# Two experts held to 192 rows, their second tile multiplied with high and low halves side by side

## The chip, the core and the metric

The program runs on one core of one Trainium2 chip. The metric is the device time of one execution in microseconds (us). Engines: PE is TensorE's matmul side and PEld its weight load, DVE is VectorE, ACT is ScalarE, POOL is GpSimd, SP only issues transfers. SBUF is the core's working memory; PSUM is the memory that matmuls write, used here in banks of 128 partitions x 512 floats.

## What is computed

Three stages on 2 x 768 tokens: banded attention, a mixture of eight experts (one expert for each token, with a sticky choice), and a gated feed-forward layer. The middle one is what the change touches:

```python
def _moe_ref(x, w_gate, w_local, w1, w2):          # x 2 x 768 x 512, 8 experts, w1 512 x 1024, w2 1024 x 512
    ...
            fresh_e = int(np.argmax(logits[b, s]))
            if s == 0 or local_gate[b, s] < 0.5:
                e = fresh_e
            else:
                e = prev_e if prev_e >= 0 else fresh_e
            prev_e = e
            ...
            h = np.maximum(x[b, s] @ w1[e], 0.0)
            out[b, s] = p[e] * (h @ w2[e])
```

Then `k = relu(xk @ w_k)`, `v = k*k @ w_v`, `out = sigmoid(xr @ w_r) * v` for all tokens.

## The kernel before, in words

**Precision.** Each operand of a large matmul is kept as two numbers, a high part (rounded for the one-pass mode F32R) and the rest, the low part; a product is three matmuls: high x high, high x low, low x high (`mm3`, lines 633 to 635). Weights arrive from DRAM in chunks of 128 x 1024 floats (512 KB, `wraw`); ACT writes the high part (`w_hi1`, line 617, two halves) and DVE the low part (`w_lo_all`, line 626, `wlo`). An expert has eight chunks: 0 to 3 for its first layer, 4 to 7 for its second.

**Places.** Routing counts the tokens of each expert and ranks them. Place `p` of the order of work (r = 0 to 7 in the code) takes the expert with rank `PLACES[p]`. Each place has a fixed number of rows, `CAPS`: the first 384, the third 320, the others 256. If an expert has more tokens than its place holds, a flag is set and the whole result is computed again by a slow general program at the end. Places 3 and 5 (`SHORT`) take the two smallest experts: 128 rows always, and 128 more behind a branch.

**One ordinary expert (r = 1, 2, 4, 6).** First layer, `l1m(r, f)` for f = 0 to 7: weights stand still, the rows of x move through (N = 256 columns, 320 at place 2), 12 matmuls for each f. ACT and DVE take relu of it and split it into high (`hh`) and low (`hl`). Second layer: for each tile of 128 rows, `l2_mm`, 24 matmuls with h standing still and 512 columns of w2 moving; then `y_out` (ACT copies the bank, ACT's queue writes it to `ys`). The third tile of place 2 has 64 rows only; for it `h3` holds high and low part next to each other as one 128-column operand, `l2_both` multiplies it by w2 high and w2 low, 16 matmuls, and `y_both` adds the two halves of the bank (ACT copies one, DVE adds, POOL's queue writes).

**What sets the order.** All is written out by hand; each engine runs its instructions in that order. Between the matmuls of an expert three kinds of small work are dealt out: `W_` issues the next split of weights of a later expert (and, through `pump`, the next loads on SP's queue); `B_` does one step of decoding the last layer's float64 weights ("words"): three DVE instructions for each piece (lines 486, 488, 490), a piece's load being asked for on POOL's queue when the piece two before it is done (`dec_load`, tiles `dwt`, two of them); and `next(late)` does one step of late routing, which turns counts into the row that each token's result has in `ys`. Tables fix how many: `BL[r]` gives `B_` for each f of the first layer and, in the second, one step at every f with `f % BL[r][1] == BL[r][1] // 2` in the first two tiles. Place 4 (`LATE`) runs late routing in place of words, and a matmul of it (line 415, operand `dj`) on PE.

The functions that the change touches:

## Time and profile before

| | us |
|---|---|
| median of three runs | 489.56 (489.03 to 489.94) |
| the profiled execution, whole | 487.52 |
| its span in the trace | 486.0 |
| PE busy in it | 468.6 (96%) |
| DVE busy | 343.7 (71%) |
| ACT busy | 264.9 (55%) |
| experts r = 1 to 7 | 154.94 to 308.05 us of the span |
| last layer | 308.05 to the end |

A matmul's row gives a start and a duration. Since matmuls are pipelined, durations overlap; what a matmul costs in a stream is the distance from its start to the next start, called its pace below. Rows of a timeline are sorted by start. The rows of the section after next are taken from several views of this one execution.

### The profile page before, as it was taken

What the parts mean: (1) busy time and instruction counts of PE and PEld (TensorE: products, weight loads), DVE (VectorE), ACT (ScalarE), POOL (GpSimd) and SP (SyncE); (2) the same over time, 40 slices, a digit from 0 to 9 for tenths busy, and PEclk for the clock granted to TensorE, in tenths of its full rate; (3) what the DMA queues carried; (4) which work ended last, traced back from release to release, by engine and by line L of the source; (5) the groups of instructions that cost most, each with busy time, mean ns of one, the idle gap of its engine ahead of it and who ended that gap; (6) DMA issues with size and microseconds to landing.
All of it is one profiled execution on the core that took longest, in us unless ns stands there. A gap on an engine that the chain in (4) does not pass through costs nothing. (4 is left out here: it accounts for less than half of the span.)

```text
span 486.0 us, 9271 instructions
## 1 busy us (share of the span) xinstructions
PE 468.6 (96%) x3227; PEld 407.2 (84%) x3227; DVE 343.7 (71%) x891; ACT 264.9 (55%) x644; POOL 112.8 (23%) x198
## 2 busy tenths in 40 slices
PE   7999999799999999999999999999999999999994
PEld 5789888678788989879879888797989899898984
DVE  7777796796957866968878968797866768263301
ACT  5877876883526745576666766862433414142320
POOL 4201212112110000000000003052663918162220
PEclk9999999999999999999999999999999999999998
DMA  8996575973685887699699842102836442200001
GB/s 185 284 223 156 146 173 169 277 230 99 252 301 185 315 260 271 196 363 329 220 332 341 273 166 77 54 2 66 325 109 233 154 160 81 72 15 23 22 3 49
DMA packets 76812, 87.42 MB, mean 180 GB/s; under 512 B 50677, under 2 KB 50933, under 8 KB 76757
## 3 DMA queue, kind: packets, MB, share of 16 engines
q1 hardware_dynamic: 68304, 63.28, 41.8%
q0 software_dynamic: 4848, 16.91, 11.0%
q10 hardware_dynamic: 3604, 6.56, 3.6%
q8 instruction: 28, 0.46, 0.4%
q14 instruction: 28, 0.22, 0.1%
HBM read 73.75 MB, written 12.98 MB: 178 GB/s over the span
## 5 line engine op out<-in xcount | busy, mean ns | idle before, releaser
L617 ACT ACTIVATE whi<-wraw 128x512 fp32r<-128x512 f32 x128 | 72.5, 623 | 7.1 <-ACTq L709 2.3
L626 DVE TENSOR_TENSOR wlo<-wraw,whi 128x1024 fp32r<-128x1024 f32 x55 | 66.1, 1218 | 4.3 <-ACT whi L617 3.8
L1456 ACT ACTIVATE sq<-S 128x256 f32<-128x256 f32 x48 | 18.5, 385 | 73.1 <-PE S L635 73.1
L633 PE MATMUL S<-xkh,whi 128*128 128x256 f32 x192 | 54.3, 283 | 0.2 <-ACT whi L617 0.2
L635 PE MATMUL S<-xkh,wlo 128*128 128x256 f32 x192 | 53.3, 278 | 0.2 <-DVE wlo L622 0.2
L634 PE MATMUL S<-xkl,whi 128*128 128x256 f32 x192 | 53.2, 277 | 0.0
L1466 POOL TENSOR_TENSOR kl<-sq,kh 128x256 fp32r<-128x256 f32 x40 | 36.0, 910 | 70.0 <-issue 36.7
L1496 DVE TENSOR_TENSOR o<-O,sig 128x512 f32<-128x512 f32 (+1 forms) x13 | 8.5, 650 | 51.0 <-PE O L635 31.8
L634 PE MATMUL O<-wlo,kh 128*128 128x512 f32 (+1 forms) x104 | 39.2, 377 | 0.3 <-DVE wlo L622 0.3
L635 PE MATMUL O<-whi,kl 128*128 128x512 f32 (+1 forms) x104 | 39.2, 377 | 0.0
L633 PE MATMUL O<-whi,kh 128*128 128x512 f32 (+1 forms) x104 | 38.9, 374 | 0.0
L633 PEld LDWEIGHTS S<-xkh,whi 128*128 128x128 f32 x192 | 36.1, 188 | 0.7 <-ACT whi L617 0.4
L635 PEld LDWEIGHTS S<-xkh,wlo 128*128 128x128 f32 x192 | 36.1, 188 | 0.4 <-DVE wlo L622 0.4
L634 PEld LDWEIGHTS S<-xkl,whi 128*128 128x128 f32 x192 | 36.2, 188 | 0.3
L1457 DVE SCALAR_TENSOR_TENSOR sq<-S,sq 128x256 f32<-128x256 f32 x48 | 20.1, 420 | 15.0 <-ACT sq L1456 14.7
L1465 ACT ACTIVATE kh<-sq 128x256 fp32r<-128x256 f32 x48 | 19.7, 412 | 12.7 <-DVE sq L1457 12.7
L635 PE MATMUL O<-whi,hl 128*128 128x512 f32 x64 | 25.1, 393 | 0.0
L634 PE MATMUL O<-wlo,hh 128*128 128x512 f32 x64 | 25.1, 392 | 0.0
L633 PE MATMUL O<-whi,hh 128*128 128x512 f32 x64 | 25.0, 391 | 0.0
L278 POOL DMA_INDIRECT xs<-X,posi x12 | 12.6, 1053 | 52.8 <-DVE acc L296 20.1
L884 ACT ACTIVATE zbig<-zbig,nm 128x232 f32<-128x232 f32 (+1 forms) x48 | 22.4, 466 | 3.7 <-DVE nm L872 3.7
L634 PEld LDWEIGHTS O<-wlo,kh 128*128 128x128 f32 x104 | 19.6, 188 | 4.6 <-DVE wlo L622 0.8
(446 smaller groups left out, 1409.1 us busy)
## 6 DMA issues: line engine op xcount, KB each, us to landing
wraw<-in_moe_w_dram SPq DMA_DIRECT2D x64, 512.0 KB, 5.2
dwt<-in_moe_w_v_dram POOLq DMA_DIRECT2D x8, 512.0 KB, 4.7
z<-in_moe_w_k_dram SPq DMA_DIRECT2D x8, 512.0 KB
z<-in_moe_w_v_dram SPq DMA_DIRECT2D x8, 512.0 KB, 5.4
ys<-yo ACTq DMA_DIRECT2D x15, 256.0 KB, 6.3
xn<-xs SPq DMA_DIRECT2D x14, 256.0 KB
vn<-in_v_dram SPq DMA_DIRECT2D x12, 256.0 KB, 3.7
dwt<-in_moe_w_k_dram POOLq DMA_DIRECT2D x6, 512.0 KB, 7.6
```

Source lines behind the costliest of these rows:

```text
L278: self.nc.gpsimd.indirect_dma_start(self.xs, bass.IndirectOffsetOnAxis(ap=self.posi[:, t:t + 1], axis=0), X[t], None)
L617: nc.scalar.activation(out=whl[r, c][0][:, sl], in_=raws[r, c][:, sl], func=ACTF.Copy)
L626: nc.vector.tensor_tensor(lo, raws.pop((r, c)), hi.bitcast(F32), op=ALU.subtract)
L633: nc.tensor.matmul(out_, lhsT=ah, rhs=bh, start=first, stop=False)
L634: nc.tensor.matmul(out_, lhsT=ah, rhs=bl, start=False, stop=False)
L635: nc.tensor.matmul(out_, lhsT=al, rhs=bh, start=False, stop=last)
L884: nc.scalar.activation(out=pe, in_=pe, func=ACTF.Exp, scale=-1.0, bias=nm[:, h:h + 1], accum_out=sm[:, h:h + 1])
L1456: nc.scalar.activation(out=sq_, in_=ps[:, 0:TB], func=ACTF.Relu)
L1457: nc.vector.scalar_tensor_tensor(sq_, ps[:, 0:TB], 0.0, sq_, op0=ALU.max, op1=ALU.mult)
L1465: nc.scalar.activation(out=hh, in_=sq_, func=ACTF.Copy)
L1466: (nc.gpsimd if b else nc.vector).tensor_tensor(hl, sq_, hh.bitcast(F32), op=ALU.subtract)
L1496: nc.vector.tensor_tensor(o[:, a:z], ps[:, 0:z - a], sig[b, i][:, a:z], op=ALU.mult)
```

## The change

Places 4 and 6 (the fifth and the seventh expert, `HALF`) hold 128 + 64 rows rather than 256. `PLACES` gives them the ranks 5 and 4 (rather than 3 and 4), and place 7, which keeps 256 rows, rank 3 (rather than 5). Their first layer has 192 moving columns; their second tile is stored as [high | low], is multiplied by `l2_both` and written by `y_both`. The relu and split of a pair of f is done in two calls (128 rows, then 64 rows). Routing gets a further small table, `second` (128 or 64), in place of the constant 128. Words: place 2 takes 8 + 8 steps rather than 6 + 6, place 6 takes 2 + 8 rather than 6 + 8. Late routing starts in the third tile of place 2 (8 steps) rather than in place 4.

```diff
-PLACES = (0, 1, 2, 7, 3, 6, 4, 5)
+PLACES = (0, 1, 2, 7, 5, 6, 4, 3)
+HALF = (4, 6)
-CAPS = [384, 256, 256 + LAST] + [256] * 5
+CAPS = [384, 256, 256 + LAST, 256, P + LAST, 256, P + LAST, 256]
...
-        nc.vector.memset(self.caps[:, 0:1], float(CAPS[0]))
-        nc.vector.memset(self.caps[:, THIRD:THIRD + 1], float(CAPS[THIRD]))
+        for r in (0, THIRD) + HALF:
+            nc.vector.memset(self.caps[:, r:r + 1], float(CAPS[r]))
...
-        for r in (1, 2):
+        for r in (1, 2) + tuple(range(HALF[0] + 1, E)):
             nc.vector.memset(self.bases[:, r:r + 1], float(BASES[r]))
...
+        self.second = c.tile([8, E], F32, name="second")
+        nc.vector.memset(self.second, float(P))
+        for r in HALF:
+            nc.vector.memset(self.second[:, r:r + 1], float(LAST))
...
-        nc.vector.tensor_scalar(nm[:, 0:1], nm[:, 0:1], -float(P), 0.0, op0=ALU.add, op1=ALU.max)
-        yield
+        yield
+        nc.vector.tensor_tensor(b8, self.R, self.second, op=ALU.mult)
+        nc.vector.tensor_reduce(nm[:, 1:2], b8, axis=AX.X, op=ALU.add)
+        yield
+        nc.vector.tensor_scalar(nm[:, 0:1], nm[:, 0:1], nm[:, 1:2], 0.0, op0=ALU.subtract, op1=ALU.max)
...
-                nc.tensor.matmul(ps, lhsT=ts_[f // 4][:, f % 4].rearrange("p s c -> p (s c)"), rhs=w[:, ds_],
+                nc.tensor.matmul(ps, lhsT=ts_[f], rhs=w[:, ds_],
...
-        return LAST if i == 2 else P
+        return LAST if i == 2 or i == 1 and r in HALF else P
...
+        if r in HALF:
+            full = pair["h"][0].rearrange("p (f s c) -> p f s c", f=2, s=2)
+            hs[r, f] = tuple(full[:, odd, j, :] for j in range(2))
+            h3[r, f] = pair["h"][1][:, odd * 2 * LAST:(odd + 1) * 2 * LAST]
+            last = pair["h"][1][:, 0:4 * LAST].rearrange("p (f s c) -> p f s c", f=2, s=2)
+            if odd:
+                both_ps = pair["ps"].rearrange("p (f c) -> p f c", f=2)
+                for t_, a, z in ((full, 0, P), (last, P, N)):
+                    relu_split(t_[:, :, 0, :], t_[:, :, 1, :], both_ps[:, :, a:z])
+            return
...
-    BL = {1: ((0, 0, 0, 0, 1, 0, 1, 0), 4), 2: ((1, 1, 1, 0, 1, 1, 1, 0), 3), 6: ((1, 1, 1, 0, 1, 1, 1, 0), 2)}
+    BL = {1: ((0, 0, 0, 0, 1, 0, 1, 0), 4), 2: ((1,) * 8, 2), 6: ((1, 0, 1, 0, 0, 0, 0, 0), 2)}
...
+                elif m == LAST:
+                    steps = l2_both(r, ps, [h3[r, f] for f in range(KF)])
...
                     if r == LATE:
                         next(late, None)
-                    elif i < 2 and f % BL[r][1] == BL[r][1] // 2:
+                    elif i == 2:
+                        next(late, None)
+                    elif f % BL[r][1] == BL[r][1] // 2:
                         B_(1)
-                if i == 2:
+                if m == LAST:
                     y_both(rp, ps, BASES[r] + TILES[r][i] * P, m)
```

Line numbers of the changed kernel are 7 or 8 higher at the places quoted below (634 for 626, 641 to 643 for 633 to 635, 681 for 673, 750 for 742, 494 to 498 for 486 to 490).

PE, place 4, the start of the second tile's second layer, before (`hh` and `hl` are high and low of h, `O` the bank):

```order
L633 MATMUL O_3663<-whi_4_3343,hh_0_3389 128x512
L634 MATMUL O_3663<-wlo_4_3344,hh_0_3389 128x512
L635 MATMUL O_3663<-whi_4_3343,hl_0_3390 128x512
L633 MATMUL O_3663<-whi_4_3343,hh_0_3389 128x512
L634 MATMUL O_3663<-wlo_4_3344,hh_0_3389 128x512
L635 MATMUL O_3663<-whi_4_3343,hl_0_3390 128x512
```

The end of the first tile and the start of the second, after; here `hh` holds both parts of the first tile and `hl` both parts of the second:

```order
L643 MATMUL O_3618<-whi_7_3541,hh_6_3576 128x512
L681 MATMUL O_3707<-whi_4_3384,hl_0_3431 128x512
L681 MATMUL O_3707<-wlo_4_3385,hl_0_3431 128x512
L681 MATMUL O_3707<-whi_4_3384,hl_0_3431 128x512
L681 MATMUL O_3707<-wlo_4_3385,hl_0_3431 128x512
```

Two matmuls stand for each f where three stood: 16 for the tile rather than 24. In the first layer the count stays, and the size changes from 128x256 to 128x192.

DVE, place 2, from the second tile's second layer to place 3's first h, before (`wlo_3` to `wlo_6` are weights of place 3; 486, 488, 490 are the three steps of a piece of words; `yo` is the third tile's result; `ehl` is the low part of place 3's h):

```order
L626 TENSOR_TENSOR wlo_3_3045<-wraw_3_2831,whi_3_3044 128x1024
L486 TENSOR_SCALAR z_2254<-dwt_3021 128x512
L626 TENSOR_TENSOR wlo_4_3077<-wraw_4_2876,whi_4_3076 128x1024
L488 SCALAR_TENSOR_TENSOR z_2254<-dwt_3021,z_2254 128x512
L490 SCALAR_TENSOR_TENSOR z_2254<-dwt_3021,z_2254 128x512
L742 TENSOR_TENSOR yo_3126<-O_3109,yo_3126 64x512
L626 TENSOR_TENSOR wlo_5_3145<-wraw_5_2937,whi_5_3144 128x1024
L626 TENSOR_TENSOR wlo_6_3162<-wraw_6_2983,whi_6_3161 128x1024
L647 TENSOR_TENSOR ehl_3135<-PT_3183,ehh_3134 128x512
```

The same stretch after, first its beginning and then its end; between them stand 12 further small instructions of late routing:

```order
L498 SCALAR_TENSOR_TENSOR z_2263<-dwt_2887,z_2263 128x512
L494 TENSOR_SCALAR z_2263<-dwt_2974 128x512
L634 TENSOR_TENSOR wlo_2_3039<-wraw_2_2838,whi_2_3038 128x1024
L496 SCALAR_TENSOR_TENSOR z_2263<-dwt_2974,z_2263 128x512
L498 SCALAR_TENSOR_TENSOR z_2263<-dwt_2974,z_2263 128x512
L634 TENSOR_TENSOR wlo_3_3058<-wraw_3_2840,whi_3_3057 128x1024
L494 TENSOR_SCALAR z_2264<-dwt_3045 128x512
L634 TENSOR_TENSOR wlo_4_3091<-wraw_4_2885,whi_4_3090 128x1024
L496 SCALAR_TENSOR_TENSOR z_2264<-dwt_3045,z_2264 128x512
L498 SCALAR_TENSOR_TENSOR z_2264<-dwt_3045,z_2264 128x512
L494 TENSOR_SCALAR z_2264<-dwt_3093 128x512
L392 TENSOR_TENSOR b_3129<-Rr,bases 8x8
```

```order
L411 TENSOR_SCALAR c_3151<-nm_3135 8x1
L413 TENSOR_SCALAR cv<-c_3151 8x1
L414 TENSOR_TENSOR cv<-cv 8x1
L418 TENSOR_SCALAR dj<-ident,cv 8x8 x3
L750 TENSOR_TENSOR yo_3167<-O_3126,yo_3167 64x512
L634 TENSOR_TENSOR wlo_5_3186<-wraw_5_2947,whi_5_3185 128x1024
L634 TENSOR_TENSOR wlo_6_3203<-wraw_6_2995,whi_6_3202 128x1024
L655 TENSOR_TENSOR ehl_3176<-PT_3224,ehh_3175 128x512
```

More steps of words, the first step of a piece (`dwt_3093`) that was first read in place 6 before, and 19 small instructions now stand in front of `yo`, the two splits and `ehl`.

## Rows read from the trace of the kernel before

**Rows 1.** The page's busy times: us, share of the span, instructions.

```profile
PE 468.6 (96%) x3227; PEld 407.2 (84%) x3227; DVE 343.7 (71%) x891; ACT 264.9 (55%) x644; POOL 112.8 (23%) x198
```

**Rows 2.** Busy time by stretch: places 2 to 4, and place 6's second layer.

```profile
core 0: us, PE busy (x) PEld busy (x) DVE busy (x) ACT busy (x) POOL busy (x), PEclk, DMA share, GB/s
179.08:208.71 29.63, 29.63 (x169) 26.97 (x168) 21.53 (x38) 15.43 (x37) 1.59 (x3) 1.00 0.79 264
208.71:222.22 13.51, 13.21 (x65) 10.39 (x64) 10.29 (x12) 12.33 (x23) 1.11 (x2) 1.00 0.97 350
222.22:246.00 23.78, 23.73 (x154) 21.38 (x155) 20.39 (x54) 13.44 (x26) 0.01 (x1) 1.00 0.83 278
271.68:282.67 10.99, 10.99 (x51) 9.02 (x49) 10.96 (x16) 5.48 (x10) 1.07 (x2) 1.00 0.83 270
```

**Rows 3.** PE's timeline (start, duration), second layer: place 2's third tile, place 4's second.

```profile
205.05 0.39 PE L673 MATMUL O<-whi,h3h 128*128 128x512 f32 x1
...
208.71 0.39 PE L633 MATMUL S<-whi,xh 128*128 128x512 f32 x1
...
240.51 0.39 PE L633 MATMUL O<-whi,hh 128*128 128x512 f32 x1
...
246.00 0.39 PE L633 MATMUL S<-whi,xh 128*128 128x512 f32 x1
```

**Rows 4.** PE's timeline: place 4's first layer, and matmuls of eight columns.

```profile
224.06 0.28 PE L633 MATMUL S<-xh,whi 128*128 128x256 f32 x1
...
225.12 0.28 PE L633 MATMUL PT<-xh,whi 128*128 128x256 f32 x1
...
71.56 0.25 PE L268 MATMUL R<-OH,tri 128*128 128x8 f32 x1
...
72.00 0.25 PE L270 MATMUL R<-acc,tri 128*128 128x8 f32 x1
```

**Rows 5.** PE's timeline around late routing's matmul in place 4.

```profile
235.51 0.40 PE L635 MATMUL O<-whi,hl 128*128 128x512 f32 x1
235.96 0.37 PE L415 MATMUL R<-dj,ones 8*128 8x24 f32 x2
```

**Rows 6.** DVE's timeline from place 2 into place 3, then PE's.

```profile
207.20 0.69 DVE L490 SCALAR_TENSOR_TENSOR z<-dwt,z 128x512 uint32<-128x512 uint32 x1
209.54 0.68 DVE L742 TENSOR_TENSOR yo<-O,yo 64x512 f32<-64x512 f32 x1 [1.65 <-ACT yo L741]
210.58 2.36 DVE L626 TENSOR_TENSOR wlo<-wraw,whi 128x1024 fp32r<-128x1024 f32 x2 [0.36 <-ACT whi L617]
214.10 0.69 DVE L647 TENSOR_TENSOR ehl<-PT,ehh 128x512 fp32r<-128x512 f32 x1 [1.16 <-ACT ehh L645]
...
215.52 0.39 PE L635 MATMUL O<-whi,ehl 128*128 128x512 f32 x1
```

**Rows 7.** The page's transfers of words: queue, count, size, us from issue to landing.

```profile
dwt<-in_moe_w_v_dram POOLq DMA_DIRECT2D x8, 512.0 KB, 4.7
dwt<-in_moe_w_k_dram POOLq DMA_DIRECT2D x6, 512.0 KB, 7.6
```

**Rows 8.** DVE: groups in place 2 (busy us, mean ns), then its timeline.

```profile
L626 DVE TENSOR_TENSOR wlo<-wraw,whi 128x1024 fp32r<-128x1024 f32 x8 | 9.7, 1219 | 0.3 <-ACT whi L617 0.3
L1323 DVE SCALAR_TENSOR_TENSOR hl<-S,hh 128x256 fp32r<-128x256 f32 x4 | 1.7, 423 | 5.3 <-ACT hh L1322 5.3
L490 DVE SCALAR_TENSOR_TENSOR z<-dwt,z 128x512 uint32<-128x512 uint32 x2 | 1.4, 692 | 0.1
L486 DVE TENSOR_SCALAR z<-dwt 128x512 uint32<-128x512 uint32 x2 | 0.8, 420 | 0.0
...
227.69 0.14 DVE L392 TENSOR_TENSOR nm<-cnt,cnt 8x1 f32<-8x1 f32 x1
...
228.36 0.15 DVE L397 TENSOR_REDUCE nm<-b 8x1 f32<-8x8 f32 x1
...
11.94 0.07 DVE L101 MEMSET caps<- 8x8 f32 x1
```

More of the change, by code (lines that the diff above doesn't have):

```diff
@@ L363, in ranks @@
         nr = pool.tile([1, 2, E], F32, name="nr")
-        nc.vector.tensor_scalar(nr[:, 0, :], ep[0:1, E:2 * E], float(P), None, op0=ALU.subtract)
+        nc.vector.tensor_tensor(nr[:, 0, :], ep[0:1, E:2 * E], self.second[0:1, :], op=ALU.subtract)
         nc.vector.tensor_tensor(nr[:, 1, :], ep[0:1, E:2 * E], self.last[0:1, :], op=ALU.subtract)
@@ L1303, in x_hi @@
         if i == 0:
-            w = 2 * P + (LAST if r == THIRD else 0)
+            w = sum(nrow(r, j) for j in range(len(TILES[r])))
             xhl[r] = tuple(xtile([P, KD, w], c, f"x{c}{r}") for c in "hl")
@@ L1683, in build @@
                 m = nrow(r, i)
-                steps = l2_both(r, ps, h3["t"]) if i == 2 else l2_mm(r, ps, i, [hs[r, f] for f in range(KF)])
+                if i == 2:
+                    steps = l2_both(r, ps, [h3["t"][f // 4][:, f % 4].rearrange("p s c -> p (s c)") for f in range(KF)])
+                elif m == LAST:
+                    steps = l2_both(r, ps, [h3[r, f] for f in range(KF)])
+                else:
+                    steps = l2_mm(r, ps, i, [hs[r, f] for f in range(KF)])
                 for f in steps:
```

## The prediction

> **What bounds the kernel now.** Read the page's head first: PE is busy 96% of the span [rows 1]. That is an average, so the second view is busy time by stretch. In places 2 and 4 PE is busy for the whole stretch or all but 0.05 us of it [rows 2], and it is the same in place 6's second layer; the granted clock there is 1.00, the 2.4 GHz level. So in the two experts that the change makes smaller, time is the number of matmuls times their pace, and a matmul taken away is time taken away. Place 3, a short expert, is the exception: PE idles 0.30 of its 13.51 us [rows 2], and there the transfers are busiest (0.97). The same view shows who comes next: DVE is busy 20.39 of 23.78 us in place 4, 21.53 of 29.63 in place 2, and 10.96 of 10.99 in place 6's second layer [rows 2]. So the third view is DVE's timeline at the seams, where the next expert first needs what DVE makes.
>
> **Second layer of the second tile (places 4 and 6).** In place 4 the 24 matmuls of the second tile run from 240.51 to 246.00: 5.49 us, 0.229 each [rows 3]. The nearest row for the new form is in the trace itself: the third tile of place 2, the same code, runs its 16 matmuls from 205.05 to 208.71: 3.66 us, also 0.229 each [rows 3]. Eight matmuls less, two places: 16 x 0.229 = **3.7 us gained**. Nothing else runs on PE there, so it is all on the path. Bounds: 3.4 to 3.7.
>
> **First layer with 192 columns.** The count stays at 96 in each place; what changes is the pace, and the trace has no F32R matmul of 192 columns. With 256 columns nine matmuls take 225.12 - 224.06 = 1.06 us, 0.118 each [rows 4]. If the pace went by columns, 192 would give 0.088. But matmuls of 8 columns with full 128-column weights, each with its own weight load, start 0.110 apart (four steps in 0.44 us [rows 4]): below some width the load of the weights sets the pace, not the columns. 0.110 to 0.112 lies just under today's 0.118, and the 8-column row is nearer to this question than the 256-column row scaled down, since both weights and mode are the same. So I take 0.112: 192 matmuls x 0.006 = **1.1 us gained**. Bounds: nothing (the pace stays 0.118) to 192 x 0.030 = 5.7 us.
> The Trainium skill, "TensorE: Matmul & The Clock Gate", section "LDWEIGHTS (loading the stationary operand)", puts a weight load at the number of its columns divided by 1.2 GHz, an estimate of 0.107 us for 128; the trace's 0.110 agrees, and by the page's figure this term would be 192 x 0.011 = 2.1 us. [...]
>
> **Late routing's matmul.** In place 4 PE waits for DVE's `dj`: 0.45 us from the matmul before it to line 415, where 0.23 is usual [rows 5]. After, `dj` is made a whole expert earlier: **0.2 us gained** (0 to 0.3).
>
> **Routing's tables.** Eight more small memsets on DVE near 12 us, at 0.065 [rows 8]: at most 0.5 us if attention's softmax, queued behind them, passes it on whole, nothing if it finds slack. I take **0.3 lost**. The extra instruction in the rank code is the same kind as the one that it replaces.
>
> **Words and late routing in place 2, and what is queued behind them.** This is the price of the change. In place 2 DVE gets four more steps of words and late routing's first eight steps, 19 small instructions. In the order after they all stand in front of `yo`, of two splits of place 3's weights and of `ehl`, which PE needs for the third matmul of place 3's second layer at 215.52 [rows 6]. Before, DVE was done with words at 207.20 + 0.69 = 207.89, waited 1.65 us to start `yo` at 209.54, did the two splits and was ready for `ehl` early enough to wait 1.16 us for ACT [rows 6]. After:
> - Two of the four steps fall in the first layer, where DVE waits 5.3 us for ACT's relu [rows 8]; I let them hide. The other two, in the second layer, are a first step (0.42) and a later one (0.69) [rows 8]; overlapped starts make them about 1.2 us together at most.
> - The 19 small instructions start 0.17 us apart (four steps from 227.69 to 228.36 [rows 8]): 19 x 0.17 = 3.2 us.
> - The piece `dwt_3045` is asked for when the third step of `dwt_2887` is done. Up to its first use stand one first step, two splits and two later steps, at start-to-start distances of about 0.4, 1.14 and 0.6: 3.9 us. A piece of `w_v` lands 4.7 us after its issue [rows 7]. DVE, in order, waits the difference, 0.8 us. (`dwt_3093` is asked for 2.7 us later and is then no later than that.)
> Sum: 1.2 + 3.2 + 0.8 = 5.2 us more work, of which 1.65 fit into the old wait: `yo` starts near 213.1. Then `yo` (0.6) and two splits (1.14 each) bring `ehl` to 216.0 and its end to 216.7, 1.2 us after PE wants it. With 0.2 for the first layer not hiding all, **1.4 us lost** in place 3. Bounds: nothing, if the wait is hidden and the small ones run closer; 4.1, if pieces land as late as the 7.6 us that the `w_k` pieces show [rows 7] (2.9 more wait, less rounding). After that stall everything in places 3 and 4 moves together, since ACT's and SP's work there follows PE's.
>
> **Edits taken at nothing.** `y_both` in places 4 and 6 adds an add on DVE (0.68 [rows 6]) and moves the write from ACT's queue to POOL's. In place 4, DVE's late routing now ends in the first tile, so DVE is free for the add; behind it on POOL stands only the memset for place 5. In place 6 the piece loads stand ahead of it on POOL and their DVE steps are done by then; the gathers behind it start after place 7's first tile. If the cover is gone, each costs up to 0.7. Relu in two calls, 128 and 64 rows: shorter instructions, more of them, about equal. In place 6 DVE loses four steps of words (2.4 us) in the first layer while PE loses 2.4 us in all, so the ratio there stays what it was; place 7 needs its fourth chunk only 2 us after its start.
>
> **Sum.** 3.7 + 1.1 + 0.2 - 0.3 - 1.4 = 3.3 us. In the profiled execution that is 487.52 - 3.3 = 484.2. The median of the runs lies 2.04 us above that execution, and nothing in the sum depends on that: 489.56 - 3.3 = **486.3 us**.
>
> **Rivals.**
> 1. *No stall in place 3.* The landing comes earlier than 4.7 us and DVE's slack takes the rest. For it: transfers are at 0.79 in place 2, not full. Gain 4.7: 484.9.
> 2. *Columns set the pace.* Against it speaks the 8-column row; for it, that 512 and 256 columns cost in proportion (0.229 and 0.118). Gain 3.3 + 4.6: 481.7. [...]
> 3. *The stall eats the gain, or more.* Place: DVE in the second layer of place 2. Price: at a landing of 7.6 us the stall is 4.1 and the gain 0.6: 489.0. It decides the sign at about 8.4 us of landing, where the stall reaches the 5.0 gained; at 10 us the stall is 6.5 and the time about 491.3. For it: two such loads in flight beside the weights' loads. Against it: eight loads of the same kind had a median of 4.7.
> 4. *F32R falls to the plain float rate under 256 columns.* Each matmul would then stream its columns four times: 4 x 192 x 0.229 / 512 = 0.34 us, + 0.226 x 192 = 43 us: about 530. No row has F32R between 8 and 256 columns, so no row excludes it.
> 5. *The change doesn't do what it says*: an expert of rank 4 or 5 with over 192 tokens would set the flag and run the general program. Working the routing out from the reference's inputs gives 324, 280, 206, 177, 172, 166, 115 and 96 tokens; 324 fits only place 0 and 280 only place 2 (the run before doesn't show the general program), so whichever expert place 1 has, ranks 4 and 5 hold 177 or less. Under 1 in 100.
>
> **How the numbers follow.** Forecast 0.52 (485 to 488), rival 1 0.17, rival 2 0.08, rival 3 0.15 (0.05 of it slower), rival 4 0.03; 0.05 is left for something slower or equal that I don't see. The two ends left out are rival 2, rival 4 and the far end of rival 3, so the range is 483.0 to 489.2. A difference under 0.2% (1.0 us) is about what a measurement of this kernel can't tell from none. Faster: 0.52 + 0.17 + 0.08 = 0.77; same: most of rival 3 and a part of the rest, 0.13; slower 0.10.
>
> **What the profile after would show.** Right: 16 rows of line 681 in the second tile of places 4 and 6, 0.229 apart; 192-column rows 0.112 apart; PE waiting 1 to 2 us for `ehl` at the start of place 3's second layer, with DVE busy without a gap ahead of it. Wrong: 192-column rows at 0.088 or above 0.118; no wait at `ehl`; a new wait of PE at the start of place 4, 6 or 7 for a `wlo`; the last layer longer than before.

## The result, and the profile after

The changed kernel takes **495.74 us** (median; 495.09 to 496.88), the kernel before, measured beside it, 489.75 us (489.03 to 490.16). The ratio is 1.0136, with a 95% interval of 1.0106 to 1.0166: slower by 1.4%, where 486.3 us was forecast and 489.2 us was the upper end of the range. Wrong in sign and in size.

The profiled execution of after took 495.09 us, with a span of 493.3. Busy time by stretch shows at once where it went; the stretches run from the first matmul of one place to the first of the next, places 1 to 7:

```profile
core 0: us, PE busy (x) PEld busy (x) DVE busy (x) ACT busy (x) POOL busy (x), PEclk, DMA share, GB/s
155.94:180.09 24.15, 23.77 (x158) 21.36 (x157) 20.79 (x27) 13.50 (x25) 2.11 (x4) 1.00 0.81 276
180.09:209.71 29.62, 29.62 (x169) 26.97 (x168) 20.38 (x37) 15.39 (x37) 2.12 (x4) 1.00 0.75 259
209.71:231.25 21.54, 15.75 (x65) 11.85 (x64) 16.30 (x36) 12.39 (x24) 1.63 (x3) 0.84 0.84 288
231.25:252.57 21.32, 21.32 (x147) 19.52 (x148) 16.21 (x42) 11.79 (x27) 0.00 (x0) 1.00 0.73 235
252.57:267.55 14.98, 13.55 (x66) 10.17 (x64) 12.89 (x16) 13.84 (x27) 1.07 (x2) 1.00 0.93 320
267.55:288.37 20.82, 20.82 (x145) 19.16 (x146) 17.58 (x27) 13.14 (x28) 1.10 (x2) 1.00 0.88 301
288.37:314.57 26.20, 25.21 (x122) 20.25 (x120) 20.12 (x36) 18.97 (x38) 5.78 (x8) 1.00 0.29 94
```

Against [rows 2]: place 4 takes 21.32 us instead of 23.78, place 6 20.82 instead of 23.16, and PE is busy from end to end in both. That is the gain, 4.8 us, as forecast. But place 3 takes 21.54 instead of 13.51 us: PE is busy for only 15.75 of it, and the granted clock is 0.84 where every other place has 1.00. Places 5 and 7, which the change doesn't touch, lose 1.47 us (14.98 for 13.51) and 0.82 us (26.20 for 25.38).

PE's timeline (start, duration) in place 3 has the wait and what follows it:

```profile
216.27 0.40 PE L642 MATMUL O<-wlo,ehh 128*128 128x512 f32 x1
222.16 0.79 PE L643 MATMUL O<-whi,ehl 128*128 128x512 f32 x1 [5.49 <-DVE ehl L655]
222.75 0.63 PE L641 MATMUL O<-whi,ehh 128*128 128x512 f32 x1
223.18 0.63 PE L642 MATMUL O<-wlo,ehh 128*128 128x512 f32 x1
...
228.18 0.40 PE L641 MATMUL O<-whi,ehh 128*128 128x512 f32 x1
228.42 0.39 PE L642 MATMUL O<-wlo,ehh 128*128 128x512 f32 x1
```

PE waits 5.49 us for `ehl`, the matmul named in the prediction, and then runs matmuls 0.43 us apart instead of 0.23 until about 227: the lower of the two clock levels, 1.2 GHz. From place 3's start to this matmul it is 12.45 us, 5.6 more than in [rows 6] (215.52 - 208.71 = 6.81); from there to place 4 it is 9.09 us instead of 6.70, so the slow clock costs another 2.4. Together that is the 8.0 us of place 3.

DVE's timeline ahead of it (start, duration, idle time before) says why `ehl` is late:

```profile
205.77 0.69 DVE L498 SCALAR_TENSOR_TENSOR z<-dwt,z 128x512 uint32<-128x512 uint32 x1
...
211.02 0.43 DVE L494 TENSOR_SCALAR z<-dwt 128x512 uint32<-128x512 uint32 x1 [3.42 <-DMA dwt<-in_moe_w_v_dram]
...
215.49 0.43 DVE L494 TENSOR_SCALAR z<-dwt 128x512 uint32<-128x512 uint32 x1 [1.58 <-DMA dwt<-in_moe_w_v_dram]
...
218.56 0.67 DVE L750 TENSOR_TENSOR yo<-O,yo 64x512 f32<-64x512 f32 x1
219.17 2.34 DVE L634 TENSOR_TENSOR wlo<-wraw,whi 128x1024 fp32r<-128x1024 f32 x2
221.43 0.67 DVE L655 TENSOR_TENSOR ehl<-PT,ehh 128x512 fp32r<-128x512 f32 x1
```

Two waits for pieces of words, 3.42 and 1.58 us, then from 215.83 to 218.56 late routing's small instructions, then `yo`, two splits and `ehl` in the order that was forecast. The transfers of these pieces (the view of the transfers, for the stretches 195 to 202, 202 to 205 and 205 to 213 us; the last number is us from issue to landing):

```profile
dwt<-in_moe_w_v_dram POOLq DMA_DIRECT2D x1, 512.0 KB, 4.0
...
dwt<-in_moe_w_v_dram POOLq DMA_DIRECT2D x1, 512.0 KB, 7.0
...
dwt<-in_moe_w_v_dram POOLq DMA_DIRECT2D x1, 512.0 KB, 8.7
```

The first piece, asked for in a lull, lands in 4.0 us; the two that DVE then waits for take 7.0 and 8.7. The median of such pieces over the whole span is still 4.8.

**What is not the change.** The profiled executions also differ in their first 155 us, before any expert. Place 1 starts at 154.94 us in the execution shown of before and at 155.94 in that of after, but at 157.38 in e4 (below), whose code up to there is that of the kernel before. In e4's execution the granted clock falls for a while inside attention (busy time from 80 to 90 us), where it is 1.00 in the other two:

```profile
80.00:90.00 10.00, 9.64 (x88) 8.68 (x87) 6.08 (x28) 6.01 (x20) 0.93 (x3) 0.83 0.90 262
```

The execution of before that was profiled is simply one of the quicker ones (487.52 against a median of 489.56). So below each kernel is read by the length of its places 1 to 7, where executions of the same code agree within some 0.2 us at places 1 and 2, and its time by the ratio. These lengths are differences between the starts of the first matmuls of neighbouring places in the trace:

| kernel | 2 | 3 | 4 | 5 | 6 | 7 | 1 to 7 | median, us | ratio to before, 95% |
|---|---|---|---|---|---|---|---|---|---|
| before | 29.63 | 13.51 | 23.78 | 13.51 | 23.16 | 25.38 | 153.1 | | 1 |
| after | 29.63 | 21.54 | 21.31 | 14.98 | 20.82 | 26.20 | 158.6 | 495.74 | 1.0136 (1.0106 to 1.0166) |
| e1 192 rows alone | 29.61 | 13.64 | 24.84 | 13.75 | 20.81 | 27.18 | 154.0 | 492.40 | 1.0075 (1.0051 to 1.0099) |
| e2 late routing back | 29.61 | 20.17 | 24.81 | 13.74 | 20.81 | 26.01 | 159.3 | 494.94 | 1.0103 (1.0044 to 1.0161) |
| e3 words back | 29.61 | 13.66 | 21.31 | 15.01 | 20.80 | 27.39 | 151.9 | 490.74 | 1.0029 (1.0004 to 1.0054) |
| e4 moves alone | 29.62 | 21.43 | 23.84 | 13.57 | 23.11 | 25.34 | 161.1 | 498.00 | 1.0171 (1.0121 to 1.0222) |
| e5 third buffer | 29.61 | 15.28 | 21.31 | 15.01 | 20.81 | 26.05 | 152.2 | 491.62 | 1.0039 (1.0005 to 1.0073) |
| e6 e5, Exp earlier | 29.62 | 16.17 | 22.03 | 13.65 | 20.81 | 25.83 | 152.3 | 490.30 | 1.0021 (0.9990 to 1.0052) |
| e7 words to place 7 | 30.33 | 13.81 | 21.31 | 13.65 | 20.81 | 27.59 | 151.7 | 490.12 | 1.0012 (0.9986 to 1.0039) |
| e8 words to place 4 | 30.34 | 13.81 | 21.31 | 13.65 | 20.80 | 26.36 | 150.4 | 488.71 | 0.9975 (0.9954 to 0.9995) |
| e9 Exp in place 4 | 29.61 | 13.66 | 21.31 | 17.75 | 20.81 | 26.11 | 153.6 | 491.51 | 1.0039 (1.0017 to 1.0061) |
| e10 write on ACT | 29.61 | 13.66 | 21.30 | 17.72 | 20.81 | 31.28 | 158.5 | 497.62 | 1.0159 (1.0133 to 1.0186) |
| e11 Exp in place 0 | 29.61 | 13.66 | 21.31 | 13.65 | 20.81 | 26.12 | 149.3 | 487.22 | 0.9944 (0.9921 to 0.9967) |
| e12 e1, relu order | 29.63 | 13.63 | 22.54 | 13.81 | 20.81 | 25.83 | 150.6 | 489.03 | 0.9977 (0.9953 to 1.0000) |
| e13 after, relu order | 29.61 | 21.72 | 21.31 | 14.30 | 20.81 | 26.57 | 158.5 | 497.29 | 1.0148 (1.0111 to 1.0184) |
| e14 e11, relu order | 29.61 | 13.66 | 21.31 | 13.65 | 20.81 | 25.47 | 148.6 | 487.84 | 0.9943 (0.9926 to 0.9961) |

The medians of before in these comparisons lie between 489.5 and 490.4 us. One of e11's ten executions took 775.66 us, with a granted clock of 0.56, and is left out of its median and ratio.

The places don't account for all of the time. In 13 of the 14 kernels with 192 rows the median lies 0.5 to 2.6 us further above that of before than the sum of the seven places says (the exception is e2, 0.7 less). No run isolates this part. Some of it may lie in the last layer, which the change doesn't touch: it took 177.99 us in the execution shown of before and 178.09 in e4's, 178.74 in after's, and 178.4 to 179.3 in the others with 192 rows, except e10's (177.91).

### The profile page after: what moved, and what is told of

It is laid out like the page before. It is cut to its first block, busy times and chain, and to the rows that moved or that the text cites. A ratio compares the mean times of both kernels' runs of the same rounds, so it can differ in the third digit from the quotient of the medians.

```text
span 493.3 us, 9261 instructions
## 1 busy us (share of the span) xinstructions
PE 468.1 (95%) x3211; PEld 405.3 (82%) x3211; DVE 343.8 (70%) x911; ACT 265.2 (54%) x652; POOL 115.3 (23%) x200
## 5 line engine op out<-in xcount | busy, mean ns | idle before, releaser
L1475 DVE SCALAR_TENSOR_TENSOR sq<-S,sq 128x256 f32<-128x256 f32 x48 | 20.1, 420 | 15.5 <-ACT sq L1474 15.1
L641 PEld LDWEIGHTS O<-whi,kh 128*128 128x128 f32 x104 | 19.6, 188 | 3.8
L643 PEld LDWEIGHTS O<-whi,kl 128*128 128x128 f32 x104 | 19.6, 188 | 3.7
L892 ACT ACTIVATE peb<-peb,nm 128x232 f32<-128x232 f32 (+1 forms) x48 | 22.2, 462 | 0.0
```

Of the source, the lines that this page charges most:

```text
L641: nc.tensor.matmul(out_, lhsT=ah, rhs=bh, start=first, stop=False)
L643: nc.tensor.matmul(out_, lhsT=al, rhs=bh, start=False, stop=last)
L892: nc.scalar.activation(out=pe, in_=pe, func=ACTF.Exp, scale=-1.0, bias=nm[:, h:h + 1], accum_out=sm[:, h:h + 1])
L1475: nc.vector.scalar_tensor_tensor(sq_, ps[:, 0:TB], 0.0, sq_, op0=ALU.max, op1=ALU.mult)
```

## The experiments

The totals that the theories of e3, e5, e7 and e8 expected came out 1 to 3 us too low, although most of their places came out as foretold; part of that is the time outside the places, above. So the places, not the totals, are what tells the theories apart.

### e1 to e4: the change taken apart

Three parts: 192 rows in places 4 and 6, words moved into place 2, late routing moved into place 2. **e1** keeps the first alone:

```diff
-    BL = {1: ((0, 0, 0, 0, 1, 0, 1, 0), 4), 2: ((1,) * 8, 2), 6: ((1, 0, 1, 0, 0, 0, 0, 0), 2)}
+    BL = {1: ((0, 0, 0, 0, 1, 0, 1, 0), 4), 2: ((1, 1, 1, 0, 1, 1, 1, 0), 3), 6: ((1, 1, 1, 0, 1, 1, 1, 0), 2)}
...
-                    elif i == 2:
-                        next(late, None)
-                    elif f % BL[r][1] == BL[r][1] // 2:
+                    elif i < 2 and f % BL[r][1] == BL[r][1] // 2:
```

> The changed kernel with the distribution of words and the place of late routing put back as they were before: places 4 and 6 hold 192 rows, nothing else differs. Theory (the 192 rows gain what was forecast, and all that is lost comes from what was moved into place 2): place 3 is back at about 13.5 us with no wait for ehl; 16 matmuls 0.23 apart and 192-column matmuls 0.112 apart in places 4 and 6 stay; the time is 4.8 us under the kernel before, less what DVE then holds back: in place 4 it has 20.39 us of work and the add of 0.68 for 21.3 us, in place 6 four steps of words more than in the change, so 0 to 3 us come back at the starts of places 5 and 7: 485 to 488. Rival (the 192 rows themselves lose somewhere, by the second relu call or the write on POOL's queue): 490 or more, with the loss in place 4, 5, 6 or 7.

Place 3 is back at 13.64 us, so the stall there does belong to the moves. But the time is 0.75% above before, the rival's figure, and my theory of e1 falls: place 4 takes 24.84 us, more than with 256 rows. PE's timeline at the old site of late routing's matmul:

```profile
237.78 0.40 PE L643 MATMUL O<-whi,hh 128*128 128x512 f32 x1
240.01 0.37 PE L423 MATMUL R<-dj,ones 8*128 8x24 f32 x2 [1.83 <-DVE dj L418]
...
241.49 0.63 PE L642 MATMUL O<-wlo,hh 128*128 128x512 f32 x1
241.92 0.63 PE L643 MATMUL O<-whi,hh 128*128 128x512 f32 x1
...
244.76 0.39 PE L641 MATMUL O<-whi,hh 128*128 128x512 f32 x1
```

PE waits 1.83 us for `dj`, with the half clock behind it (matmuls 0.43 apart from 241.49 to 244.48). In the kernel before it didn't wait there: the 0.45 us of [rows 5] run from one matmul's start to the next one's, and DVE had finished `dj` (235.34 + 0.48 = 235.82) before the matmul ahead ended (235.51 + 0.40 = 235.91):

```profile
235.34 0.48 DVE L410 TENSOR_SCALAR dj<-ident,cv 8x8 f32<-8x8 f32 x3
```

Place 7 loses 1.8 us too, waiting for its first `ehl` behind the words of place 6. So the moves were not free to be left out: they pay 3.5 us in place 4 (24.84 to 21.31) and about 1 in place 7, and cost 8 in place 3.

**e2** undoes the late routing's move alone (the second half of e1's diff), **e3** the words' move alone (the first half).

> The change with late routing's first eight steps back in place 4; the words stay moved. Theory (place 3's 8.0 us are 5.0 us of waits for two pieces of words, 2.7 of late routing and 1.2 of two added word steps on DVE, less 1.65 of slack, and on top some 2 us of PE at the half clock after the wait): without late routing DVE is ready for ehl 2.7 us earlier, PE's wait there falls from 5.5 to about 3, place 3 takes 17 to 19 us, and the time is 490.5 to 493. Rival 1 (late routing is the whole loss): place 3 is back near 13.5 and the time is under 488.5. Rival 2 (the waits for the pieces are so long that late routing ran in their shadow, it stands behind the last of them, so this needs a later landing): place 3 stays above 20 us and the time above 494.

Place 3 takes 20.17 us and the time is 494.94: rival 2's figures, though not quite for its reason. Late routing stands behind the last piece and ran in nobody's shadow; but in the execution shown the two pieces landed later still, 8.1 and 9.9 us after their issue, DVE waited 6.2 instead of 5.0 us for them, and PE 4.0 instead of 5.5 for `ehl`. That execution is the slowest of four (497.92 us; the others 492.92 to 496.28), so how much of the stall is late routing's isn't settled by e2. Place 4 shows the same 24.81 as e1.

> The change with the words distributed as before; late routing stays in place 2's third tile. Theory: the word pieces are asked for as in the kernel before, DVE doesn't wait for them in place 2, and late routing's 2.7 us stand against 1.65 us of slack: PE waits about 1 us for ehl, too short for the clock to fall, place 3 takes 14.5 to 15.5 us; place 6 has four word steps more on DVE and may give back up to 2 us in place 7: 486 to 489. Rival 1 (late routing alone makes the stall): place 3 above 18 us, 492 or more. Rival 2 (the pieces land late whatever is asked for, since places 2 and 3 carry the most transfers): DVE still waits over 2 us at line 494 in place 2.

Place 3 takes 13.66 us: with the words as before, late routing's 2.7 us in place 2 cost 0.15 us. No wait of PE for `ehl` is left in place 3. DVE doesn't wait for a piece, and not because they land early (the transfers of e3, stretches 199 to 205 and 205 to 215 us):

```profile
dwt<-in_moe_w_v_dram POOLq DMA_DIRECT2D x1, 512.0 KB, 3.8
...
dwt<-in_moe_w_v_dram POOLq DMA_DIRECT2D x1, 512.0 KB, 7.8
```

The second one, asked for at 206.65 us, takes 7.8 us here too; but nobody needs it before place 6. The kernel before has the same piece at the same point of place 2; nobody waits for it there, and its trace has no landing for it. Places 5 (15.01) and 7 (27.39) keep their losses. Even so the seven places together are 1.2 us shorter than before, while the median lies 1.2 us above that of before, and 1.7 us over the theory's upper end; the places don't explain that.

**e4** puts both moves on the kernel before, with 256 rows.

> The kernel before, with 256 rows in places 4 and 6 as it has them, and only the two moves: words distributed as in the change, late routing's first eight steps in place 2's third tile. Theory (the loss belongs to the moves and not to the 192 rows): place 3 takes 20 to 22 us instead of 13.5, place 4 is shorter by 0.2, and the time is the kernel before plus 7 to 8: 496.5 to 498. Rival (the stall needs the 192 rows as well, for instance their other gather or their other order of loads): 489 to 493.

498.00 us, place 3 at 21.43: the theory's figures. DVE waits 5.0 us for the two pieces and PE 5.1 for `ehl`. The 192 rows have no part in the stall.

### e5: is it the wait for the pieces?

```diff
-            for j in PIECES[TAILED + k_ + 2:TAILED + k_ + 3]:
-                dec_load(j, dw_tile())
+            for j in PIECES[TAILED + k_ + 3:TAILED + k_ + 4]:
+                dec_load(j, ring[k_ % 3])
...
-        dec_load(PIECES[TAILED], dw_tile())
+        ring = [dw_tile(), dw_tile(), zs[7]]
+        dec_load(PIECES[TAILED], ring[0])
         pump(4)
-        dec_load(PIECES[TAILED + 1], dw_tile())
+        dec_load(PIECES[TAILED + 1], ring[1])
+        dec_load(PIECES[TAILED + 2], ring[2])
```

> The change with a third buffer for the pieces of words (the memory of chunk 7, which is written last, serves as one until then), so that each piece is asked for three pieces ahead instead of two; order of DVE's work as in the change. Theory (5.0 us of the stall are DVE's waits for pieces that were asked for too late): DVE no longer waits at line 494 in place 2, late routing and the added word steps remain, 3.9 us against 1.65 us of slack; PE's wait for ehl falls from 5.5 to 0 to 2.3 us, place 3 takes 13.6 to 16 us instead of 21.5, and the time is 488 to 490.5. Rival (the pieces land late because the transfers are full there, not because they are asked for late): DVE waits as long as before, place 3 stays above 19 us and the time above 493; a third piece in flight could also delay the weights' loads, seen as ACT waiting for wraw.

DVE's order of work is that of the change, only the pieces are asked for one earlier. Of the 5.0 us of waits 0.65 is left, PE waits 1.07 us for `ehl`, the clock holds, and place 3 takes 15.28 us: 6.3 of the 8.0 us are gone. The pieces still take 7.1 and 8.9 us to land, so the waits go because the pieces are asked for earlier, not because they land faster.

```profile
211.92 0.43 DVE L494 TENSOR_SCALAR z<-dwt 128x512 uint32<-128x512 uint32 x1 [0.65 <-DMA dwt<-in_moe_w_v_dram]
...
218.60 0.51 PE L643 MATMUL O<-whi,ehl 128*128 128x512 f32 x1 [1.07 <-DVE ehl L655]
```

### e6 to e9 and e11: places 5 and 7, and where DVE has room

In after, ACT's timeline at the seam from place 4 into place 5:

```profile
251.24 0.28 ACT L459 ACTIVATE pex<-pex 128x96 f32<-128x96 f32 x1 [3.72 <-DVE pex L458]
...
257.33 0.60 ACT L665 ACTIVATE ha5h<-S 128x512 f32<-128x512 f32 x1
```

The Exp of the probabilities, which follows late routing, holds ACT for 3.72 us until DVE gets to `pex`; behind it in ACT's order stand splits and place 5's `ha5h`, for which PE waits 1.13 us. **e6** moves it ahead in place 4, on top of e5:

```diff
-        yield from n.late_route(rp, mp)
-        yield from n.probs(mp)
+        g = n.late_route(rp, mp)
+        for _ in range(8):
+            yield next(g)
+        yield from n.probs(mp)
+        yield from g
```

> As the run with the third buffer, and the probabilities are taken ahead of the rest of late routing in place 4: their four steps come right after the eight that stand in place 2, so at the start of place 4's first layer instead of the end of its second. Theory (place 5 lost 1.5 us because ACT's Exp of the probabilities stood 3.7 us in ACT's queue waiting for DVE, with the weights' splits and ha5h behind it): place 5 falls from 15.0 to about 13.5 us, the wait of the Exp to under 1.5 us, and the time is 1 to 1.5 us under the run with the third buffer alone. Rival (place 5 waits because DVE itself is late with wlo at that seam): place 5 stays at 14.5 or more.

Place 5 falls to 13.65 us, as the theory has it. But late routing's matmul now comes later among PE's and waits 0.70 us: place 4 takes 22.03. The intervals of e5 and e6 overlap. In place 3 (16.17 us) PE waits longer for `ehl` than in e5, and the granted clock of that place is still 1.00; the matmuls behind the wait stand 0.23 us apart (PE's timeline):

```profile
218.85 0.50 PE L643 MATMUL O<-whi,ehl 128*128 128x512 f32 x1 [1.97 <-DVE ehl L655]
219.18 0.39 PE L641 MATMUL O<-whi,ehh 128*128 128x512 f32 x1
219.41 0.40 PE L642 MATMUL O<-wlo,ehh 128*128 128x512 f32 x1
```

**e7** gives place 2 its old words, place 6 the light ones of the change, and the probabilities go to place 2; **e8** also puts the four steps left over into the second tile of place 4 (the last line, which e7 doesn't have); `prb` is the generator of the probabilities, which late routing no longer ends with:

```diff
-    BL = {1: ((0, 0, 0, 0, 1, 0, 1, 0), 4), 2: ((1,) * 8, 2), 6: ((1, 0, 1, 0, 0, 0, 0, 0), 2)}
+    BL = {1: ((0, 0, 0, 0, 1, 0, 1, 0), 4), 2: ((1, 1, 1, 0, 1, 1, 1, 0), 3), 6: ((1, 0, 1, 0, 0, 0, 0, 0), 2)}
...
                     B_(BL[r][0][f])
+                    if r == THIRD and f in (1, 3, 5, 7):
+                        next(prb, None)
...
                     if r == LATE:
                         next(late, None)
+                        B_(i == 1 and f % 2)
```

> The change with words in place 2 as before (12 steps) and in place 6 as in the change (10 steps), so that four steps fall to place 7; late routing's first eight steps stay in place 2's third tile; the probabilities' four steps stand in place 2's first layer, at chunks 1, 3, 5 and 7. Theory (each loss beside the gain of the 192 rows has its own cause: words in place 2 make place 3's stall, words in place 6 the 2.0 us of place 7, the Exp the 1.5 us of place 5): places 3 and 5 take 13.5 to 14 us, place 4 21.3, place 6 20.8, place 7 25.4 to 26.5; places 1 to 7 together 148.5 to 150.5 us against 153.1 before, and the time 485 to 487. Rival (four steps more in place 7 cost there what they save at its start, or the probabilities bring back the stall in place 3): 488 or more.

> As the run before it, with the four steps of words put into the second tile of place 4's second layer (DVE stood idle 4.6 of 21.3 us in that place when words were as before). Theory: DVE takes them in its idle time, the places are as in the run before it and place 7 is free of them: 484.5 to 486.5. Rival (idle time that stands ahead of the seam can't be used: DVE comes late with the splits and ehl of place 5, the more since transfers are at 0.97 there): place 5 takes 15 us or more and the time is 487 or more.

Places 3 to 6 come out as foretold in both, the totals don't. The probabilities cost 0.7 us in place 2 (30.3), which neither theory had. In e7 place 7 pays for the words (27.59, the rival); in e8 place 4 takes them for nothing, and e8 is the first of these that is faster than before: 0.9975.

**e9** takes the probabilities out of place 2 and puts them into place 4, behind late routing's matmul (as in e6, with 11 for 8), with e8's words.

> The change with words in place 2 as before (12 steps), in place 6 as in the change (10), and four in the second tile of place 4's second layer; late routing's first eight steps in place 2's third tile as in the change; the probabilities' four steps come right after the matmul of late routing and its copy, so in place 4's first layer, and the rest of late routing after them. Theory (each loss has its own place, and DVE's idle time in place 4's first layer can take the probabilities, where place 2's could not: it took 0.7 us there): place 2 takes 29.6 us, place 3 13.7, place 4 21.3, place 5 13.65, place 6 20.8, place 7 26.2, together with place 1 149.4 us against 153.1 before; the time is 3 to 3.7 us under the kernel before: 486 to 487. Rival (the probabilities delay the first layer's split of relu in place 4, or the words still late at the seam make place 5 wait): place 4 or 5 longer by 0.7 or more and the time within 0.3% of the kernel before.

The rival, and worse than it said: place 2 is back at 29.61, but place 5 takes 17.75 us. PE waits 1.8 us for place 5's `ehl`, and the granted clock of that place is 0.90. Place 4 takes the words without loss (e8), but not the words and the probabilities together. **e11** puts the probabilities into place 0 instead, where DVE stands idle for 3.9 us:

```diff
             B_(B0[u])
+            if u in (2, 3, 4, 5):
+                next(prb, None)
```

> As the run with four words steps in place 4's second tile and the probabilities in place 2 (e8), but the probabilities' four steps stand in place 0's first tile, where DVE has a gap of 3.9 us. Theory (a step is free only where DVE has no work queued behind it that the next seam waits for): place 2 is back from 30.3 to 29.6 us, places 3 to 7 stay as in that run (13.8, 21.3, 13.65, 20.8, 26.2), places 1 to 7 together 149.5 to 150 us against 153.1 before, and the time is 2.5 to 3 us under the kernel before. Rival (the order in place 4 with words in its second tile was at its limit there, and any shift makes place 5 wait as in the run with probabilities in place 4): place 5 over 15 us, and the time at or above the kernel before.

As the theory has it: places 2 to 6 lose no more than 0.15 us each against before (stretches of e11, places 2 to 7), and the kernel takes 487.22 us, 0.56% less than before (0.33 to 0.79) and 1.9% less than the change as it was made.

```profile
181.37:210.98 29.61, 29.61 (x169) 26.97 (x168) 22.22 (x44) 15.41 (x37) 1.58 (x3) 1.00 0.76 262
210.98:224.64 13.66, 13.36 (x66) 10.24 (x64) 11.94 (x26) 12.34 (x24) 1.60 (x3) 1.00 1.00 366
224.64:245.95 21.31, 21.31 (x147) 19.52 (x148) 17.14 (x39) 13.25 (x28) 0.00 (x0) 1.00 0.77 269
245.95:259.60 13.65, 13.35 (x66) 10.25 (x64) 12.88 (x16) 12.43 (x24) 1.63 (x3) 1.00 1.02 373
259.60:280.41 20.81, 20.81 (x145) 19.15 (x146) 17.56 (x27) 13.15 (x28) 1.09 (x2) 1.00 0.86 303
280.41:306.53 26.12, 25.32 (x122) 20.25 (x121) 20.04 (x36) 18.97 (x38) 5.72 (x8) 1.00 0.32 95
```

### e10: the write on POOL's queue

On top of e9, place 6's second tile is written from ACT's queue (`q` is `nc.scalar` there):

```diff
-        nc.gpsimd.dma_start(out=ys[row:row + m, :], in_=yo[0:m, :])
+        (q or nc.gpsimd).dma_start(out=ys[row:row + m, :], in_=yo[0:m, :])
```

> As the run before it, with place 6's second tile written to memory from ACT's queue, as in the kernel before, instead of POOL's. Theory (place 7 takes 26.2 instead of 25.4 us because the gathers of the result on POOL's queue, which PE waits for at the end of place 7, stand behind that write): place 7 takes 25.4 to 25.6 us and the time is 0.6 to 0.8 us under the run before it. Rival (the write is long done by then, it was issued some 11 us ahead of the first gather, and the gather's own data land later for another reason): place 7 stays at 26 us or more; ACT may then wait for DVE's add in front of the write and be late for place 7's ehh, up to 1 us more.

The second half of the rival, five times as dear: place 7 takes 31.28 us. The write is ACT's to issue, the data are DVE's (ACT's timeline, place 6 into 7):

```profile
290.81 0.51 ACTq L751 DMA_DIRECT2D ys<-yo  x1
291.35 1.28 ACT L1730 ACT_TABLE_LOAD   x1 [4.53 <-DVE yo L750]
```

ACT stands 4.53 us for DVE's add, and PE then 3.74 us for ACT's `hn` with the half clock behind it. The write on POOL's queue is what makes the second tile's form cheap here. PE's wait for the gathered rows at the end of place 7 is still 0.55 us, so the write on POOL's queue isn't shown to be behind that.

### e12 to e14: the relu in two calls

In places 4 and 6 of after, ACT's second relu of a pair waits for DVE's first subtraction, and DVE then waits 0.34 us for the second relu, once per pair of chunks. Both read the same bank of PSUM, which is the likely reason; the trace shows only the waits (ACT's timeline, then DVE's):

```profile
245.17 0.28 ACT L1330 ACTIVATE hl<-PT 128x128 fp32r<-128x128 f32 x1 [1.22 <-DVE hh L1331]
...
245.48 0.29 DVE L1331 SCALAR_TENSOR_TENSOR hl<-PT,hl 128x128 fp32r<-128x128 f32 x1 [0.34 <-ACT hl L1330]
```

**e12** is e1 with the order turned:

```diff
-                for t_, a, z in ((full, 0, P), (last, P, N)):
-                    relu_split(t_[:, :, 0, :], t_[:, :, 1, :], both_ps[:, :, a:z])
+                parts = [(t_[:, :, 0, :], t_[:, :, 1, :], both_ps[:, :, a:z]) for t_, a, z in ((full, 0, P), (last, P, N))]
+                for a_, _, src in parts:
+                    nc.scalar.activation(out=a_, in_=src, func=ACTF.Relu)
+                for a_, b_, src in parts:
+                    nc.vector.scalar_tensor_tensor(b_, src, 0.0, a_.bitcast(F32), op0=ALU.max, op1=ALU.subtract)
```

> As the run with the 192 rows alone (words and late routing where they were before), but of each pair of chunks ACT's two relu calls stand first and DVE's two subtractions after them, where each subtraction stood behind its own relu and the second relu waited for the first subtraction. In that run DVE comes 15.1 us after the start of place 4 to dj, before it was 13.1; PE waits 1.8 us for it, runs at half the clock after that, and place 4 takes 24.8 instead of 21.3 us. Theory (the relu in two calls, which I took at nothing, makes dj late: 0.34 us of idle DVE per pair and four pairs): DVE comes to dj about 1.3 us earlier, PE waits under 0.6 us, the clock doesn't fall, place 4 takes 21.3 to 22 us and the time is 488.5 to 490. Rival (dj is late because PE gets to it 1.2 us earlier with DVE's other work unchanged, and the order in the pair does nothing): place 4 stays above 24 us and the time above 491.5.

DVE comes to `dj` 14.4 us after the place's start instead of 15.1 (0.7 earlier, not 1.3), PE waits 1.16 us instead of 1.83 (PE's timeline), and the clock doesn't fall:

```profile
239.71 0.37 PE L423 MATMUL R<-dj,ones 8*128 8x24 f32 x2 [1.16 <-DVE dj L418]
240.01 0.50 PE L641 MATMUL O<-whi,hh 128*128 128x512 f32 x1
240.35 0.39 PE L642 MATMUL O<-wlo,hh 128*128 128x512 f32 x1
```

Place 4 takes 22.54 us, 2.3 less than e1, and place 7 25.83, 1.35 less. So with nothing moved at all the 192 rows alone come out at 0.9977, at the edge of what can be told from no change. The theory had the direction and the time; its 0.34 us per pair are half as much in the end.

> The change with the order in relu's pairs as in the run before (ACT's two calls first, then DVE's two subtractions), nothing else. It tells how much of the loss of the change belongs to the two calls, with words and late routing where the change puts them. Theory (the two calls cost DVE 0.34 us per pair, of which in place 4 the Exp at its end gets 0.7 to 1.3 us and in place 6 the start of place 7 gets some; place 3 comes before the first of these pairs): place 3 stays at 20 to 22 us, place 5 falls from 15.0 to 13.7 to 14.5, place 7 from 26.2 to 25.4 to 26.1, and the time is 493.5 to 495. Rival (with late routing in place 2 the pairs hide, as the first layers of places 4 and 6 are PE's alone): places 5 and 7 stay as they are and the time as well, 495 to 496.5.

Place 5 takes 14.30 us, 0.7 less: the Exp now comes 2.0 us ahead of place 5 instead of 1.3. Place 7 doesn't gain (26.57), and the ratio, 1.0148, can't be told from after's 1.0136. About half of place 5's loss goes with the relu's order; all of it goes when the probabilities are taken earlier (e6).

> The fastest arrangement so far (e11: words in place 2 as before, 10 in place 6, four in place 4's second tile, probabilities in place 0) with the order in relu's pairs as in the run before. Theory (there places 4 to 6 are at PE's pace already, 21.3, 13.65 and 20.8 us, so DVE's gain goes into slack; only place 7's 0.7 us, the wait for the gathered rows, could move): places 2 to 6 as in e11, place 7 25.5 to 26.1, the time 0 to 0.6 us under e11's, so 0.5 to 0.7% under the kernel before. Rival (ACT's two calls in a row delay its weights' splits, and place 4 or 6 loses): one of them 0.5 us longer or more.

Places 2 to 6 as in e11; place 7 takes 25.47 us, and PE waits 0.26 us for the gathered rows there instead of 0.80. The ratio, 0.9943 (0.9926 to 0.9961), can't be told from e11's. The best of these kernels are e11 and e14, 0.6% under the kernel before.

## Why the prediction was wrong, step by step

- **What bounds the kernel.** Right where it said so: places 4 and 6 are PE's alone, and a matmul taken away is time taken away. The two places gained 4.8 us of the 5.0 in the sum. The 16 matmuls of the second tile in place 4 run from 248.90 to 252.57: 3.67 us, 0.229 each, as [rows 3] had promised.

```profile
248.90 0.39 PE L681 MATMUL O<-whi,hl 128*128 128x512 f32 x1
...
252.57 0.39 PE L641 MATMUL S<-whi,xh 128*128 128x512 f32 x1
```

- **192 columns.** Right. Thirteen matmuls from 231.53 to 232.98 us are 0.112 apart, the value taken from the 8-column row of [rows 4]: at 8 and at 192 columns the pace is the same, so the columns don't set it there, and the load of 128 weight columns, which both have, fits. Rivals 2 (0.088) and 4 (0.34) are excluded. The estimate by the Trainium skill, "TensorE: Matmul & The Clock Gate", section "LDWEIGHTS (loading the stationary operand)", 0.107 us for such a load, is near it.

```profile
231.53 0.27 PE L643 MATMUL S<-xh,wlo 128*128 128x192 f32 x1
...
232.98 0.28 PE L641 MATMUL S<-xh,whi 128*128 128x192 f32 x1
```

- **Words and late routing in place 2.** The mechanism was right, the seam and even the matmul; the price was 1.4 us where it is 8.0. This is the step that failed, and it is rival 3, which had the point of decision at landings of 8.4 us. Three numbers of that step held: 3.9 us from the first piece's issue to DVE's need of it (3.6), late routing 3.2 us (2.7), `yo` to `ehl` 2.9 (2.87). The others:
  1. *The landing.* I took 4.7 us as the median of eight pieces over the whole span [rows 7]; the two that counted took 7.0 and 8.7. Their first wait was 3.4 us instead of 0.8. The median stands on six of the eight: the pieces that were asked for in place 2's second layer, at 198.34 and 204.25 us, have no landing in the trace of before. The rows at hand spoke against it: place 3, into which the landings fall, has a DMA share of 0.97 [rows 2], and I had read that number for another purpose. Of the weights' loads, as large and asked for in the same stretch, one has a landing, and it took 9.3 us (the view below). e5 isolates it: with the wait down to 0.65 us, close to the 0.8 that I had put in, place 3 loses 1.8 us, close to the 1.4 that I had put out.
  2. *The second piece.* "Is then no later than that", I wrote; DVE waited another 1.6 us for it, since it was issued 2.8 us later into the same traffic and took longer.
  3. *The clock.* The sum had a wait and no price for what comes after it. 2.4 of the 8.0 us are matmuls at the lower clock behind the wait of 5.5 us.

Transfers asked for from 202 to 214 us, before (the last number, where there is one, is us from issue to landing; a count without one has no landing in the trace):

```profile
wraw<-in_moe_w_dram SPq DMA_DIRECT2D x6, 512.0 KB, 9.3
...
dwt<-in_moe_w_v_dram POOLq DMA_DIRECT2D x1, 512.0 KB
```

These three make 2.6 + 1.6 + 2.4 = 6.6 us, as much as lies between 1.4 and 8.0; smaller differences (late routing 0.5 us cheaper, for one) cancel. (In rival 3 the time for a landing of 10 us follows as 491.1, not 491.3.)

- **Edits taken at nothing.** Two were not nothing. "DVE's late routing now ends in the first tile, so DVE is free" was wrong: DVE ran 3.7 us behind the program's order at the end of place 4, and ACT's Exp stood in its own queue for that long (place 5, +1.5; e6 and e13 show it). "Relu in two calls, 128 and 64 rows: shorter instructions, more of them, about equal" counted durations and not the waits of ACT and DVE for each other; e12 shows it to be worth 2.3 us at the old site of late routing.
- **Late routing's matmul.** Misread: PE doesn't wait for `dj` in the kernel before (e1's section). The move gained 0.1 us, not 0.2: from the matmul ahead of it to the second one behind it PE takes 0.63 us more than two steps of its pace before, and 0.51 more after. What I didn't ask is what the old site would cost with 192 rows, 3.5 us (e1 against e3). The sum of the change is hardly touched by that, but whoever would have undone the move on my figures would have lost more than I said.
- **Routing's tables.** 0.3 us taken; nothing of it can be told from the scatter of the first 155 us.
- **Place 7.** +0.8 us in after. PE waits there 0.99 us for rows gathered by POOL; the second of the four gathers takes 5.0 us from issue to landing, and 3.5 in e4, where that wait is 0.21. The place is 25.34 in e4, 25.8 to 26.6 in most kernels with 192 rows, 25.47 in e14. Neither the write on POOL's queue (e10) nor the order of relu (e13) is shown to be behind it; its cause stays open.

In the profiled executions: -4.8 (places 4 and 6) + 8.0 + 1.5 + 0.8 = +5.5 us for places 1 to 7; the first 155 us add 1.0 and the last layer 0.75, and whether these belong to the change isn't shown. The medians differ by 6.0.

## What to carry to other kernels

Read a transfer's landing from the stretch in which the moved request will be in flight, with the DMA share of that stretch, and not from a median over the span; look which transfers the median stands on, since those in question may have no landing in the trace, and at loads of the same size beside them. Work that is moved on an in-order engine is free only where that engine has a gap ahead of the next seam: the same four steps cost 0.7 us in place 2, 4 in place 4 beside the words, and nothing in place 0. And price a wait of PE with the slow matmuls that can stand behind it.

## What the runs showed of the hardware

- Transfers of 512 KB from POOL's queue landed 3.6 to 9.9 us after their issue in these kernels. In after one took 4.0 us in a stretch with a DMA share of 0.42 (195 to 202 us), and one 8.7 in a stretch with 0.95 (205 to 213); those asked for from 204 to 209 us in after and e2 to e5 took 7.0 to 9.9. Loads from SP's queue beside them were as late, 9.3 us in before and 9.5 in after. What delays them is not isolated.
- After waits of 5.5 (after), 1.84 (e2), 1.83 (e1) and 1.80 us (e9) PE's matmuls ran 0.43 us apart for some 3 to 5 us, the granted clock at 1.2 GHz. After waits of 1.97 (e6), 1.59 (e1, place 7), 1.16 (e12) and 1.07 us (e5) they ran on at 0.23. So the length of the wait alone doesn't tell whether the clock falls. In e12 place 4 is 2.3 us shorter than in e1: 0.7 us of wait, and 1.6 of matmuls at the lower clock.
- An F32R matmul with its own 128-column weights starts 0.112 us after the one before it at 8 and at 192 columns alike.
